# The second MLP of an attention and two-MLP kernel: its TensorE order written out, its token operands double buffered, all weights streamed, and its cosine without a magnitude step

## The chip, the cores and the metric

The kernel runs on one core of a Trainium2 chip. The core has TensorE (PE in the profile; its weight loads are PEld), VectorE (DVE), ScalarE (ACT), GpSimd (POOL) and SyncE (SP, which only issues DMAs here). The metric is the device time of one launch in microseconds; lower is better. The kernel before takes 1585.07 us, the median of three runs (1583.58 to 1586.71).

## The reference

Three stages follow each other: packed attention, an MLP with `h * sigmoid(h)`, and a second MLP with `h * cos(h)`.

```python
p_packed = sm_attn(p, k, v)          # 8 batches, 8 heads, 32 packed queries, 576 keys, head_dim 64
attn_out = sm_attn(q, p_packed, p_packed)
x = attn_out.transpose(0, 2, 1, 3).reshape(4608, 512)

h = x @ w_in                         # first MLP: 512 -> 2048
g = h * (1.0 / (1.0 + np.exp(-h)))
x = g @ w_out                        # 2048 -> 512

h = x @ w_in                         # second MLP, with weights of its own
g = h * np.cos(h)
out = (g @ w_out).astype(np.float32) # 4608 x 512
```

The four weight matrices arrive as 64-bit floats and are decoded on the chip.

## The kernel before

**Arithmetic.** An fp32 operand is split into a rounded part and a remainder, and a product of two such operands is three matmuls into one PSUM bank (`mm3`: remainder times rounded, rounded times remainder, rounded times rounded). `split` makes the two parts: a cast on ACT or DVE, then a subtraction on DVE or POOL.

**Planner.** Nothing is issued when it is written. Every operation is recorded with its cost, its reads and writes (a PSUM bank counts as a whole), and a due time; a list scheduler (`Plan.schedule`, `Plan.order`) then gives each engine one fixed order. Where two engines can do an operation (`either`), the scheduler chooses. Each engine runs its order strictly, so an operation that waits holds up all that stand behind it on that engine. SP issues the DMAs in one such order too.

**First MLP.** 256 steps, each for 288 tokens and 128 of the 2048 hidden columns: six matmuls into a bank `hb`, tanh on ACT, a multiply and a split into `g` on DVE, ACT or POOL, and three steps later twelve matmuls (288 columns wide) into the four banks `acc`. Attention and the decoding of weights run beside it. Its results go to DRAM (`ydram`, and `ypart` for the first two batches, whose sum is made in four parts).

**Second MLP.** Nine blocks of 2 x 256 tokens, eight steps a block, 72 steps in all. A step computes two hidden chunks of 128 columns for both token halves as seven block products instead of eight (`second`). Each product is six matmuls of 256 columns, so a step has 42. `x` and `y` are two PSUM banks of a step: products 0 and 1 go into the halves of x, ACT copies x1 to y1 and x2 to `m`; products 2 and 3 add to y1 and x1, DVE forms x2 = y1 + m; products 4 and 5 add to y1 and x2, DVE forms y2 = y1 + m; product 6 adds to y1. Both banks then go through the cosine (`half_second`): ACT rounds h/2pi to an integer `n`, DVE subtracts that multiple of 2pi in two instructions and clamps, ACT takes the magnitude and then the sine, DVE multiplies by h, and a split gives `g`. The projection of each bank is twelve matmuls of 512 columns into the four banks `acc`, so a step has 24 of them. Steps alternate between two pairs of banks.

**Operands.** The seven token operands of a block (fourteen tiles, `yt`) are sums and differences of four token quarters, loaded from DRAM into `raw` and split (`put` in `load_y`). They lie in a ring of 20 slots, so those of products 0 to 2 of the next block can be made early (`AHEAD_Y = 3`), and the others only in the last step of the block, as each product frees its slots. The weights of product 0 stay on the chip (`held`, eight tiles); those of products 1 to 6 are read again for every block through a ring of 16 slots, 256 KB each (`load_unit`). For three blocks the parts in `ypart` are added first, each through one of two buffers `yad`.

**Order around the change.** Projections get due times 1.6 and 2.1 steps after their step's start, products 0 to 0.95; within these the scheduler interleaves them. `plan.margin = 400` adds 400 ns to what it allows between another engine and TensorE.

## Time and profile before

| | |
|---|---|
| median of three runs | 1585.07 us |
| profiled execution, its own time | 1586.77 us |
| its span, first to last instruction | 1584.7 us |
| PE busy | 1540.7 us, 97% |
| PEld busy | 1378.6 us, 87% |
| DVE busy | 1145.0 us, 72% |
| ACT busy | 857.7 us, 54% |
| POOL busy | 269.0 us, 17% |
| mean granted TensorE clock | 0.991 |

Shares of busy time are means over the whole span. A matmul's duration includes the filling and draining of the array, which overlap with its neighbours, so a dense stretch is read from how far apart matmuls start and not from their durations. Idle time of an engine that nobody waits for costs nothing. Names in the rows: `hb`, `mb`, `sb` are the banks of the products, `acc` those of the projection, `g` the split result of an activation, `r` and `n` the tiles of the cosine, `y` and many `w` tiles hold token operands and weights of the second MLP (tiles that held first-MLP operands are used again). All operations are recorded through one helper, so all stand on one line (L206 before, L207 in the changed kernel).

### The profile page before, as it was taken

What the parts mean: (1) busy time and instruction counts of PE and PEld (TensorE: products, weight loads), DVE (VectorE), ACT (ScalarE), POOL (GpSimd) and SP (SyncE); (2) the same over time, 40 slices, a digit from 0 to 9 for tenths busy, and PEclk for the clock granted to TensorE, in tenths of its full rate; (3) what the DMA queues carried; (4) which work ended last, traced back from release to release, by engine and by line L of the source; (5) the groups of instructions that cost most, each with busy time, mean ns of one, the idle gap of its engine ahead of it and who ended that gap; (6) DMA issues with size and microseconds to landing.
All of it is one profiled execution on the core that took longest, in us unless ns stands there. A gap on an engine that the chain in (4) does not pass through costs nothing.

```text
span 1584.7 us, 31208 instructions
## 1 busy us (share of the span) xinstructions
PE 1540.7 (97%) x11642; PEld 1378.6 (87%) x11642; DVE 1145.0 (72%) x2149; ACT 857.7 (54%) x1798; POOL 269.0 (17%) x294
## 2 busy tenths in 40 slices
PE   9889999999999999999999999999999999999998
PEld 7678878999879998899988898888889898889887
DVE  4997657564787879687657768787777767686766
ACT  5875544344454565556556555555555555555554
POOL 0231001020131303130202203132212102020100
PEclk9899999999999999999999999999999999999999
DMA  9677365222765567565877647666565545464551
GB/s 248 204 227 187 106 146 125 68 46 40 153 210 175 172 175 171 181 202 189 273 245 226 202 147 227 199 191 207 168 186 168 175 151 187 154 186 150 163 164 36
DMA packets 295639, 270.51 MB, mean 171 GB/s; under 512 B 165440, under 2 KB 214080, under 8 KB 295488
## 3 DMA queue, kind: packets, MB, share of 16 engines
q1 hardware_dynamic: 295488, 268.52, 57.1%
q8 instruction: 92, 1.51, 0.4%
q14 instruction: 59, 0.48, 0.1%
HBM read 215.22 MB, written 53.22 MB: 169 GB/s over the span
## 4 chain that ended last, share of the span: by engine, by line
PE 75%; DVE 14%; DMA 4%; ACT 3%; issue 2%; POOL 1%; SPq 1%; DVEq 0%; ACTq 0%; POOLq 0%
PE acc L206 41%; PE hb L206 21%; PE mb L206 7%; PE sb L206 6%; DVE r L206 4%; DVE g L206 1%; DMA yad<-ypart 1%; ACT r L206 1%; DVE w L206 1%; DVE y L206 1%; SPq L206 1%; DVE raw L206 1%; DVE wy L206 1%; DVE wd L206 1%; DVE gf L206 1%
## 5 line engine op out<-in xcount | busy, mean ns | idle before, releaser
L206 PE MATMUL acc<-w,g 128*128 128x512 f32 x1728 | 472.9, 395 | 4.8 <-DVE g L206 4.4
L206 PE MATMUL acc<-g,w 128*128 128x288 f32 x3072 | 470.2, 298 | 4.9 <-ACT ysb L206 3.1
L206 PEld LDWEIGHTS acc<-g,w 128*128 128x128 f32 x3072 | 426.0, 189 | 31.4 <-issue 20.8
L206 PEld LDWEIGHTS acc<-w,g 128*128 128x128 f32 x1728 | 301.1, 189 | 50.2 <-DVE g L206 7.4
L206 PE MATMUL hb<-a,w 128*128 128x288 f32 x1536 | 261.4, 301 | 9.5 <-ACT a L206 3.9
L206 PEld LDWEIGHTS hb<-a,w 128*128 128x128 f32 x1536 | 221.7, 190 | 30.0 <-issue 11.2
L206 PE MATMUL hb<-y,w 128*128 128x256 f32 x1056 | 183.9, 283 | 3.3 <-DVE r L206 2.8
L206 ACT CAST g<-gf 128x288 fp32r<-128x288 f32 x231 | 100.0, 434 | 153.6 <-PE acc L206 114.5
L206 POOL TENSOR_TENSOR g<-gf,g 128x288 fp32r<-128x288 f32 x83 | 82.1, 991 | 546.7 <-ACT g L206 472.2
L206 PEld LDWEIGHTS hb<-y,w 128*128 128x128 f32 x1056 | 161.4, 191 | 14.0 <-DVE r L206 3.6
L206 DVE SCALAR_TENSOR_TENSOR gf<-gf,hb 128x288 f32<-128x288 f32 x256 | 114.0, 447 | 50.6 <-ACT gf L206 49.3
L206 ACT ACTIVATE gf<-hb 128x288 f32<-128x288 f32 x256 | 104.6, 410 | 74.9 <-PE hb L206 67.0
L206 DVE TENSOR_TENSOR g<-gf,g 128x288 fp32r<-128x288 f32 x173 | 83.7, 485 | 83.1 <-ACT g L206 80.3
L206 ACT ACTIVATE r<-r 128x512 f32<-128x512 f32 x144 | 91.0, 632 | 86.1 <-DVE r L206 85.6
L206 DVE TENSOR_TENSOR g<-r,g 128x512 fp32r<-128x512 f32 x135 | 97.5, 722 | 44.6 <-ACT g L206 44.2
L206 ACT CAST g<-r 128x512 fp32r<-128x512 f32 x134 | 83.6, 624 | 71.6 <-DVE r L206 71.2
L206 PE MATMUL hb<-w,w 128*128 128x256 f32 x672 | 117.4, 282 | 2.2 <-DVE r L206 1.3
L206 PEld LDWEIGHTS hb<-w,w 128*128 128x128 f32 x672 | 103.9, 190 | 10.5 <-DVE r L206 1.5
L206 DVE SCALAR_TENSOR_TENSOR r<-n,r 128x512 f32<-128x512 int32 x144 | 105.6, 733 | 3.0
L206 ACT ACTIVATE r<-r,half_pi 128x512 f32<-128x512 f32 x144 | 104.2, 724 | 3.1
L206 ACT ACTIVATE n<-hb 128x512 int32<-128x512 f32 x72 | 43.1, 598 | 88.2 <-PE hb L206 87.9
L206 PE MATMUL mb<-y,w 128*128 128x256 f32 x408 | 74.6, 284 | 2.8 <-DVE hb L206 1.7
(212 smaller groups left out, 2062.8 us busy)
## 6 DMA issues: line engine op xcount, KB each, us to landing
w<-w2s SPq DMA_DIRECT2D x440, 256.0 KB, 3.5
w2s<-wd SPq DMA_DIRECT2D x28, 512.0 KB, 3.6
wd<-in_moe_w_in SPq DMA_DIRECT2D x24, 512.0 KB, 5.0
w<-w1dram SPq DMA_DIRECT2D x48, 256.0 KB, 3.0
wd<-in_moe_w_out SPq DMA_DIRECT2D x20, 512.0 KB, 4.6
ydram<-ysb SPq DMA_DIRECT2D x64, 144.0 KB, 2.9
raw<-ydram SPq DMA_DIRECT2D x72, 128.0 KB, 3.3
w2dram<-wd SPq DMA_DIRECT2D x16, 512.0 KB, 3.0
```

Source lines behind the costliest of these rows:

```text
L206: run = lambda: emit(*[real(x) for x in args], **{k: real(x) for k, x in kw.items()})
```

## The change

1. **Order.** `plan.inorder` makes each matmul of the second MLP wait for the one before it, as written. A written step `s` is: products 0 and 1; the projection of the x bank of step s-2 (twelve matmuls); products 2 and 3; half of the projection of its y bank (six); products 4 and 5; the other half; product 6. Steps 0 and 1 alternate without projections, and two more steps hold the last projections. The margin of 400 ns is no longer set there, and all due times of a step are one. The other engines are still ordered by the scheduler.
2. **Projection inner order.** The twelve matmuls go round the four banks three times (rounded part of `g` times both parts of the weight first, the remainder of `g` last), except for the last hidden chunk. In the first MLP the same is done for all but a block's last chunk.
3. **Token operands.** 28 slots instead of 20, so two blocks fit; all of `put` for a block is recorded at once. The slots come from the weight tiles that held product 0, and from `gf`, `g` and `ysb` tiles of the first MLP (`m`, `yad` and three slots).
4. **Weights.** All seven units of a step are loaded through the same ring of 16 slots.
5. **Cosine.** `n` is rounded from h/2pi + 0.25, so the sine's argument needs no magnitude; one ACT instruction per half step goes. `r`, `g2` and `o` have four buffers (three, three and two before).
6. x takes the banks `mb` and `sb`, y the banks `hb`; two dummy matmuls that opened the y banks go.

```diff
--- before.py
+++ after.py
...
@@ -237,6 +238,9 @@
                 self.block = True
         i = len(self.ops) - 1
         waits = set()
+        if engine == self.PE and self.inorder is not None:
+            waits.update(self.inorder)
+            self.inorder = [i]
         for r in filter(None, ins):
             if r[1] is None:
 
@@ -877,9 +881,10 @@
         PAIR.append(len(steps))
     NS = len(steps)
     LAG = 3
...
@@ -907,9 +912,16 @@
         g = gs()[:, :, :n]
         split(g, t)
         plan.due = due_first(s + LAG + 0.5)
-        for dm in range(KC):
-            c = slice(dm * P, dm * P + P)
-            mm3(acc[dm][:, :n], (W[fc][:, 0, c], W[fc][:, 1, c]), (g[:, 0], g[:, 1]), begin, end)
+        chunks = [slice(dm * P, dm * P + P) for dm in range(KC)]
+        if end:
+            for dm, c in enumerate(chunks):
+                mm3(acc[dm][:, :n], (W[fc][:, 0, c], W[fc][:, 1, c]), (g[:, 0], g[:, 1]), begin, end)
+        else:
+            for dm, c in enumerate(chunks):
+                for j in (1, 0):
+                    T.matmul(acc[dm][:, :n], W[fc][:, j, c], g[:, 0], start=begin and j == 1, stop=False)
+            for dm, c in enumerate(chunks):
+                T.matmul(acc[dm][:, :n], W[fc][:, 0, c], g[:, 1], start=False, stop=False)
         plan.due = None
         if end:
             t0 = k0 // HALF % 2 * (2 * S if part else NT) // 2 + (2 * pr + k0 // S) * HALF
@@ -927,31 +939,27 @@
     order = list(range(3, 6)) + [0, 1, 2] + list(range(6, NBLK))
     wout = {}
     yt = {}
-    X, Y = hb, [mb, sb]
+    X, Y = [mb, sb], hb
 
...
     raws, raw = lates("raw", F32, 10, TB)
-    yads, yad = lates("yad", F32, 2, TB)
-    m5s, m5ring = lates("m5", F32, 2, TB)
-    ys, _ = lates("y", F32R, 12, TB)
+    yad = ring([t[:, :TB] for t in ysb_tiles])
+    m5ring = ring([t[:, :TB] for t in gf_tiles])
+    ys, _ = lates("y", F32R, 9, TB)
     ns, nring = lates("n", I32, 2)
-    rs_, rring = lates("r", F32, 3)
-    g2s, g2ring = lates("g2", F32R, 3)
-    os_, oring = lates("o", F32, 2)
+    rs_, rring = lates("r", F32, 4)
+    g2s, _ = lates("g2", F32R, 4)
+    os_, oring = lates("o", F32, 4)
 
     halves = [W[FC + kc * 4 + s][:, i] for s in range(4) for kc in range(2) for i in range(2)]
     halves += [W[FC + 8 + kc * 4 + s][:, i] for s in range(4) for kc in range(2) for i in range(2)]
...
-    yring = ring(ys + [as_y(x) for x in halves[0:2] + halves[26:32]])
-    held = halves[2:4] + halves[20:26]
-    uring = ring(halves[4:16] + halves[16:20])
-
-    AHEAD_Y = 3
-    later = {}
+    yring = ring(ys + [as_y(x) for x in halves[0:5] + halves[21:32]] + [t[:, :, :TB] for t in g_tiles])
+    uring = ring(halves[5:21])
 
     def load_y(i):
 
...
@@ -1001,71 +1008,103 @@
         DMA.dma_start(f32(w).rearrange("p (k t f) -> p k t f", k=2, t=2), w2s[fp // 4, prod, :, fp % 4])
         return as_w(w)
 
-    def half_second(s, fc, h):
-
-        i = s // FH
+    def cosine(h, g):
+
         n = nring()
-        A.activation(n, h, AF.Copy, scale=INV_2PI / WEIGHT)
+        A.activation(n, h, AF.Copy, scale=INV_2PI / WEIGHT, bias=0.25)
         r = rring()
         V.scalar_tensor_tensor(r, n, -TWO_PI_HI * WEIGHT, h, op0=ALU.mult, op1=ALU.add)
         V.scalar_tensor_tensor(r, n, -TWO_PI_LO * WEIGHT, r, op0=ALU.mult, op1=ALU.add)
-        V.tensor_scalar(r, r, 4.0 * WEIGHT, -4.0 * WEIGHT, op0=ALU.min, op1=ALU.max)
-        A.activation(r, r, AF.Abs)
-        A.activation(r, r, AF.Sin, scale=-1.0 / WEIGHT, bias=half_pi)
+        V.tensor_scalar(r, r, 1.570796 * WEIGHT, -4.7123885 * WEIGHT, op0=ALU.min, op1=ALU.max)
+        A.activation(r, r, AF.Sin, scale=1.0 / WEIGHT, bias=half_pi)
         V.tensor_tensor(r, r, h, ALU.mult)
-        g = g2ring()
         split(g, r)
-        w = wout[fc]
-        last = fc == FC - 1
-        for t in range(4):
-            plan.due = due_second(s + (2.1 if fc >= FH else 1.6))
-            c = slice(t * P, t * P + P)
-            mm3(acc[t], (g[:, 0, c], g[:, 1, c]), (w[:, 0], w[:, 1]), fc == 0, last)
-            plan.due = None
+        return g
+
...
+    gt, st, m5s = {}, {}, {}
+
+    def project(s, x, part):
+
+        if not 0 <= s < NS2:
+            return
+        i, fp = divmod(s, FH)
+        fc = fp + x * FH
+        g, w = gt[s, x], wout[fc]
+        if fc == FC - 1:
+            passes = [(t, a, b) for t in range(4) for a, b in ((1, 0), (0, 1), (0, 0))]
+        else:
+            passes = [(t, 0, b) for b in (1, 0) for t in range(4)] + [(t, 1, 0) for t in range(4)]
+        for n, (t, a, b) in list(enumerate(passes))[6 * part : 6 * part + 6]:
+            first = fc == 0 and n < 4
+            last = fc == FC - 1 and n % 3 == 2
+            T.matmul(acc[t], g[:, a, t * P : (t + 1) * P], w[:, b], start=first, stop=last)
             if last:
-                o = oring()
-                if t % 2:
-                    V.tensor_scalar(o, acc[t], WEIGHT**-2, None, op0=ALU.mult)
-                else:
-                    A.activation(o, acc[t], AF.Copy, scale=WEIGHT**-2)
-                p0 = order[i] * TB + t % 2 * P
-                cuts = [p0] + list(range(p0 // HALF * HALF + HALF, p0 + P, HALF)) + [p0 + P]
-                for a, b in zip(cuts, cuts[1:]):
-                    r0 = a // HALF * S + t // 2 * HALF + a % HALF
-                    DMA.dma_start(out[r0 : r0 + b - a, :], o[a - p0 : b - p0])
-
-    def second(s):
-
-        i, fp = divmod(s, FH)
+                output(i, t)
+
+    def product(s, prod, dst, start=False):
+
+        i = s // FH
+        w = st[s][prod]
+        for c in range(2):
+            b = yt[i, prod, c]
+            mm3(dst, (w[:, c, 0], w[:, c, 1]), (b[:, 0], b[:, 1]), start and c == 0, c == 1, skip_group_check=True)
+
+    def multiply(s, k):
+
+        if s >= NS2:
+            return
         x, y = X[s % 2], Y[s % 2]
         x1, x2, y1, y2 = x[:, :TB], x[:, TB:], y[:, :TB], y[:, TB:]
-        ws = [held[fp]] + [uring() for _ in range(6)]
-        ws = [as_w(ws[0]) if i else load_unit(ws[0], fp, 0)] + [load_unit(w, fp, j) for j, w in enumerate(ws) if j]
-
-        def product(prod, dst, start, due):
-            plan.due = due_second(s + due)
-            for c in range(2):
-                b = yt[i, prod, c]
-                w = ws[prod]
-                mm3(dst, (w[:, c, 0], w[:, c, 1]), (b[:, 0], b[:, 1]), start and c == 0, c == 1, skip_group_check=True)
-            plan.due = None
-            if fp == FH - 1 and i + 1 < NBLK and prod + AHEAD_Y < 7:
-                later[i + 1](prod + AHEAD_Y)
-
-        m5 = m5ring()
-        product(0, x1, True, 0)
-        product(1, x2, False, 0.1)
-        A.copy(y1, x1)
-        A.copy(m5, x2)
-        product(2, y1, False, 0.35)
-        product(3, x1, False, 0.45)
-        V.tensor_tensor(x2, y1, m5, ALU.add)
-        product(4, y1, False, 0.6)
-        product(5, x2, False, 0.7)
-        V.tensor_tensor(y2, y1, m5, ALU.add)
-        half_second(s, fp, x)
-        product(6, y1, False, 0.95)
-        half_second(s, fp + FH, y)
+        if k == 0:
+            st[s] = [load_unit(uring(), s % FH, j) for j in range(7)]
+            m5s[s] = m5ring()
+            product(s, 0, x1, True)
+            product(s, 1, x2)
+            A.copy(y1, x1)
+            A.copy(m5s[s], x2)
+        elif k == 1:
+            product(s, 2, y1)
+            product(s, 3, x1)
+            V.tensor_tensor(x2, y1, m5s[s], ALU.add)
+        elif k == 2:
+            product(s, 4, y1)
+            product(s, 5, x2)
+            V.tensor_tensor(y2, y1, m5s[s], ALU.add)
+            gt[s, 0] = cosine(x, g2s[2 * s % 4])
+        else:
+            product(s, 6, y1)
+            gt[s, 1] = cosine(y, g2s[2 * s % 4 + 1])
+
+    def second(s):
+
+        plan.due = due_second(s)
+        if s == 1:
+            for k in range(4):
+                for x in range(2):
+                    multiply(x, k)
+        elif s > 1:
+            multiply(s, 0)
+            project(s - 2, 0, 0)
+            project(s - 2, 0, 1)
+            multiply(s, 1)
+            project(s - 2, 1, 0)
+            multiply(s, 2)
+            project(s - 2, 1, 1)
+            multiply(s, 3)
+        plan.due = None
 
 
 
@@ -1173,16 +1212,11 @@
         if more:
             seconds(b0 + 3)
 
-    change(top, [att], "yp", "right", raws + yads + m5s + ys)
...
     load_y(0)
-    for prod in range(AHEAD_Y, 7):
-        later[0](prod)
-    for x in Y:
-        yd = yt[0, 0, 0]
-        T.matmul(x[:, :TB], yd[:, 0, :P], yd[:, 0], start=True, stop=True)
-    plan.margin = plan.MARGIN
-    for s in range(NS2):
+    plan.inorder = []
+    for s in range(NS2 + 2):
         i, fp = divmod(s, FH)
         if i == 0:
             for x in range(2):
```

TensorE at a change of block, in the kernel before: the first products of a new block (`y0`, `y1`) into `hb0`, among the last products of the old block into `hb1` and projection matmuls into `acc`.

```order
L206 MATMUL acc0_88<-w2_98,g21_8871 128x512
L206 MATMUL mb_94<-w31_1868,w28_103 128x256
L206 MATMUL hb0_92<-y0_8651,w17_1138 128x256 x3
L206 MATMUL hb0_92<-y1_8652,w17_1138 128x256 x3
L206 MATMUL acc1_89<-w2_98,g21_8871 128x512
L206 MATMUL acc2_90<-w2_98,g21_8871 128x512
L206 MATMUL acc3_91<-w2_98,g21_8871 128x512
L206 MATMUL hb1_93<-y10_8661,w25_1140 128x256
L206 MATMUL hb1_93<-y11_8662,w25_1140 128x256 x2
L206 MATMUL mb_94<-y2_8653,w17_1138 128x256 x3
L206 MATMUL mb_94<-y3_8654,w17_1138 128x256 x3
L206 MATMUL hb1_93<-y11_8662,w25_1140 128x256
```

TensorE in the middle of a step of the changed kernel: products 2 and 3 of the step (into `hb0`, then `mb`), six projection matmuls of the step before the last, then products 4 and 5 begin.

```order
L207 MATMUL hb0_92<-w26_1148,w18_1146 128x256 x3
L207 MATMUL hb0_92<-w30_1149,w18_1146 128x256 x3
L207 MATMUL mb_94<-w30_1149,w22_1147 128x256 x3
L207 MATMUL mb_94<-w27_1838,w22_1147 128x256 x3
L207 MATMUL acc0_88<-w9_1143,g21_8921 128x512
L207 MATMUL acc1_89<-w9_1143,g21_8921 128x512
L207 MATMUL acc2_90<-w9_1143,g21_8921 128x512
L207 MATMUL acc3_91<-w9_1143,g21_8921 128x512
L207 MATMUL acc0_88<-w9_1143,g21_8921 128x512
L207 MATMUL acc1_89<-w9_1143,g21_8921 128x512
L207 MATMUL hb0_92<-w27_1838,w22_1147 128x256 x3
L207 MATMUL hb0_92<-w31_1839,w22_1147 128x256 x3
```

The old order was chosen matmul by matmul; the new one is the written pattern, the same in every step.

DVE in the last step before the same change of block, kernel before: `hb1<-sb,m` and `sb<-sb,m` are the sums x2 and y2, the `r` rows the cosine, and the `raw`, `y0`, `y1` and `y2` rows make the token operands that the block which starts next reads.

```order
L206 SCALAR_TENSOR_TENSOR r1_8868<-n0_8865,hb1_93 128x512
L206 TENSOR_TENSOR sb_95<-sb_95,m51_8650 128x256
L206 SCALAR_TENSOR_TENSOR r1_8868<-n0_8865,r1_8868 128x512
L206 TENSOR_TENSOR raw0_8637<-raw2_8639,raw0_8637 128x256
L206 TENSOR_SCALAR r1_8868<-r1_8868 128x512
L206 TENSOR_TENSOR raw8_8645<-raw6_8643,raw0_8637 128x256
L206 TENSOR_TENSOR y0_8651<-raw0_8637,y0_8651 128x256
L206 CAST y2_8653<-raw8_8645 128x256
L206 CAST y1_8652<-raw1_8638 128x256
L206 TENSOR_TENSOR y2_8653<-raw8_8645,y2_8653 128x256
L206 SCALAR_TENSOR_TENSOR r2_8869<-n1_8866,sb_95 128x512
L206 TENSOR_TENSOR r1_8868<-r1_8868,hb1_93 128x512
```

DVE two steps before the same change of block, changed kernel: the cosine of both banks, among it token operands (`raw`, `w29`, `w30`), and at the end the sum x2 of the next step (`sb<-hb1,gf1`).

```order
L207 TENSOR_TENSOR r0_8916<-r0_8916,mb_94 128x512
L207 SCALAR_TENSOR_TENSOR r1_8917<-n1_8915,r1_8917 128x512
L207 TENSOR_TENSOR raw1_8362<-raw3_8364,raw1_8362 128x256
L207 TENSOR_SCALAR r1_8917<-r1_8917 128x512
L207 TENSOR_TENSOR g20_8920<-r0_8916,g20_8920 128x512
L207 TENSOR_TENSOR w29_1141<-raw0_8361,w29_1141 128x256
L207 TENSOR_TENSOR raw8_8369<-raw6_8367,raw0_8361 128x256
L207 TENSOR_TENSOR r1_8917<-r1_8917,hb0_92 128x512
L207 TENSOR_TENSOR raw3_8364<-raw7_8368,raw3_8364 128x256
L207 CAST w30_1149<-raw4_8365 128x256
L207 TENSOR_TENSOR w30_1149<-raw9_8370,w30_1149 128x256
L207 TENSOR_TENSOR sb_95<-hb1_93,gf1_149 128x256
```

As many token rows as before stand among the cosine rows near a change of block, but in the changed kernel they serve a block that starts eight steps later (their slots have just come free), and the sums x2 and y2 stand right behind the cosine's rows or between token rows.

## Rows read from the trace of the kernel before

**Rows 1.** Chain that ended last: start us, us, what.

```profile
303.32 1.59 PE acc L206 x12
...
990.83 1.92 PE hb L206 x16
...
1297.75 1.61 PE acc L206 x7
```

**Rows 2.** Timeline of PE: start us, us, what, matmuls, idle before.

```profile
790.05 1.59 PE L206 MATMUL hb<-y,w 128*128 128x256 f32 x12
...
1575.27 5.51 PE L206 MATMUL acc<-w,g 128*128 128x512 f32 x23 [0.24 <-DVE g L206]
```

**Rows 3.** Groups by line, 790.3 to 806 us, PE: busy us, mean ns.

```profile
L206 PE MATMUL acc<-g,w 128*128 128x288 f32 x36 | 5.7, 295 | 0.0
```

**Rows 4.** Windows: PE, PEld, DVE, ACT, POOL busy (x), PEclk, DMA, GB/s.

```profile
858.00:898.00 40.00, 37.66 (x222) 33.26 (x221) 32.36 (x58) 21.47 (x43) 14.02 (x17) 0.96 0.64 200
...
898.00:944.00 46.00, 46.00 (x290) 41.46 (x289) 30.93 (x55) 23.86 (x44) 0.92 (x1) 1.00 0.49 160
...
1384.00:1424.00 40.00, 38.24 (x237) 33.74 (x236) 32.73 (x60) 22.15 (x44) 9.82 (x12) 1.00 0.58 179
...
1471.00:1511.00 40.00, 39.80 (x250) 35.77 (x249) 28.68 (x53) 21.13 (x41) 6.07 (x7) 1.00 0.55 172
...
1511.00:1557.00 46.00, 46.00 (x291) 41.51 (x290) 31.16 (x55) 24.95 (x46) 0.00 (x0) 1.00 0.38 121
```

**Rows 5.** Waits of PE from 789 us on: us in total, times, longest.

```profile
PE acc L206 <- DVE g L206: 4.4, 9, 1.8
...
PE hb L206 <- DVE r L206: 4.0, 3, 1.8
...
PE mb L206 <- DVE hb L206: 2.7, 3, 1.0
...
PE hb L206 <- DVE hb L206: 1.5, 2, 0.9
```

**Rows 6.** Timeline, 879 to 888 us: POOL, DVE and PE.

```profile
879.59 1.86 POOL L206 TENSOR_TENSOR raw<-raw,yad 128x256 f32<-128x256 f32 x2
...
880.79 1.21 DVE L206 TENSOR_TENSOR g<-r,g 128x512 fp32r<-128x512 f32 x1
...
882.05 1.79 PE L206 MATMUL acc<-w,g 128*128 128x512 f32 x5 [1.78 <-DVE g L206]
```

**Rows 7.** Groups by line, whole span: busy us, mean ns, idle before.

```profile
L206 ACT ACTIVATE n<-hb 128x512 int32<-128x512 f32 x72 | 43.1, 598 | 88.2 <-PE hb L206 87.9
...
L206 DVE SCALAR_TENSOR_TENSOR r<-n,hb 128x512 f32<-128x512 int32 x72 | 49.2, 684 | 16.6 <-ACT n L206 16.1
...
L206 DVE SCALAR_TENSOR_TENSOR r<-n,r 128x512 f32<-128x512 int32 x144 | 105.6, 733 | 3.0
...
L206 DVE TENSOR_SCALAR r<-r 128x512 f32<-128x512 f32 x144 | 68.3, 475 | 3.2
...
L206 ACT ACTIVATE r<-r 128x512 f32<-128x512 f32 x144 | 91.0, 632 | 86.1 <-DVE r L206 85.6
...
L206 ACT ACTIVATE r<-r,half_pi 128x512 f32<-128x512 f32 x144 | 104.2, 724 | 3.1
...
L206 DVE TENSOR_TENSOR r<-r,hb 128x512 f32<-128x512 f32 x72 | 49.2, 684 | 11.9 <-ACT r L206 11.4
...
L206 ACT CAST g<-r 128x512 fp32r<-128x512 f32 x134 | 83.6, 624 | 71.6 <-DVE r L206 71.2
...
L206 DVE TENSOR_TENSOR g<-r,g 128x512 fp32r<-128x512 f32 x135 | 97.5, 722 | 44.6 <-ACT g L206 44.2
...
L206 DVE TENSOR_TENSOR hb<-mb,m 128x256 f32<-128x256 f32 x36 | 15.4, 428 | 9.0 <-PE hb L206 8.8
```

**Rows 8.** Waits of PE up to 789 us.

```profile
PE acc L206 <- POOL g L206: 1.8, 2, 1.4
```

**Rows 9.** DMA issues: count, KB each, median us to landing.

```profile
w<-w2s SPq DMA_DIRECT2D x440, 256.0 KB, 3.5
```

More of the change, by code (lines that the diff above doesn't have):

```diff
@@ L107, in __init__ @@
         self.margin = 0
+        self.inorder = None
         self.block = None
@@ L879, in attention_mlps_kernel @@
     LAG = 3
-    gfs = ring(tiles(gp, [P, TA], F32, "gf", 2))
-    gs = ring(tiles(gp, [P, 2, TA], F32R, "g", LAG))
-    ysbs = ring(tiles(gp, [P, TA], F32, "ysb", 2))
+    gf_tiles = tiles(gp, [P, TA], F32, "gf", 2)
+    g_tiles = tiles(gp, [P, 2, TA], F32R, "g", LAG)
+    ysb_tiles = tiles(gp, [P, TA], F32, "ysb", 2)
+    gfs, gs, ysbs = ring(gf_tiles), ring(g_tiles), ring(ysb_tiles)
     def first(s):
@@ L990, in put @@
                 split(yt[i, prod, c], x[c])
-        for prod in range(AHEAD_Y):
+        for prod in range(7):
             put(prod)
-        later[i] = put
     def load_wout2(c, w):
@@ L1037, in second, with output @@
-    def second(s):
-        i, fp = divmod(s, FH)
+        return g
+    def output(i, t):
+        o = oring()
+        if t % 2:
+            V.tensor_scalar(o, acc[t], WEIGHT**-2, None, op0=ALU.mult)
+        else:
+            A.activation(o, acc[t], AF.Copy, scale=WEIGHT**-2)
+        p0 = order[i] * TB + t % 2 * P
+        cuts = [p0] + list(range(p0 // HALF * HALF + HALF, p0 + P, HALF)) + [p0 + P]
+        for a, b in zip(cuts, cuts[1:]):
+            r0 = a // HALF * S + t // 2 * HALF + a % HALF
+            DMA.dma_start(out[r0 : r0 + b - a, :], o[a - p0 : b - p0])
@@ L1057, in second @@
-        product(1, x2, False, 0.1)
-        A.copy(y1, x1)
-        A.copy(m5, x2)
-        product(2, y1, False, 0.35)
-        product(3, x1, False, 0.45)
-        V.tensor_tensor(x2, y1, m5, ALU.add)
-        product(4, y1, False, 0.6)
-        product(5, x2, False, 0.7)
-        V.tensor_tensor(y2, y1, m5, ALU.add)
-        half_second(s, fp, x)
-        product(6, y1, False, 0.95)
-        half_second(s, fp + FH, y)
+        if k == 0:
[14 more added lines that the diff above has]
+            gt[s, 0] = cosine(x, g2s[2 * s % 4])
+        else:
+            product(s, 6, y1)
+            gt[s, 1] = cosine(y, g2s[2 * s % 4 + 1])
@@ L1174, in attention_mlps_kernel @@
             seconds(b0 + 3)
-    change(top, [att], "yp", "right", raws + yads + m5s + ys)
+    change(top, [att], "yp", "right", raws + ys)
     change(mid, [a2p], "cp", "left", ns + rs_ + g2s + os_)
     load_y(0)
-    for prod in range(AHEAD_Y, 7):
-        later[0](prod)
-    for x in Y:
-        yd = yt[0, 0, 0]
-        T.matmul(x[:, :TB], yd[:, 0, :P], yd[:, 0], start=True, stop=True)
-    plan.margin = plan.MARGIN
-    for s in range(NS2):
+    plan.inorder = []
+    for s in range(NS2 + 2):
         i, fp = divmod(s, FH)
```

## The prediction

> **What bounds the kernel now.** I read the chain that ended last first: PE holds 75% of it, most of that in the projection banks `acc` and the product banks `hb`, and its dense pieces give PE's pace [rows 1]: twelve matmuls of 288 columns in 1.59 us are 132.5 ns each, sixteen of 256 columns in 1.92 us are 120 ns, seven of 512 columns in 1.61 us are 230 ns. Then the timeline of PE gives the ends of the second MLP [rows 2]: its first product starts at 790.05 us, and the last 23 matmuls start at 1575.27 and take 5.51, so it ends at 1580.78. That is 790.7 us.
>
> What must fit there: a step has 42 product matmuls (42 x 0.120 = 5.04 us) and 24 projection matmuls (24 x 0.230 = 5.52), together 10.56 us, and 72 steps are 760.3 us. In the same stretch lie 36 matmuls left over from the first MLP [rows 3], 36 x 0.1325 = 4.8 us, and two dummies, 0.24. Sum 765.3. So PE loses 790.7 - 765.3 = 25.4 us in the second MLP, and this is all that a better order there can win.
>
> Where it loses them, the windows say [rows 4]. Between changes of block PE is busy in every microsecond (46.00 of 46 in the first such stretch and in the last). In the 40 us around a change it is idle for 2.34 us at the first (40 - 37.66), 1.76 at the one near 1404 and 0.20 at the last. DVE and POOL show why: in the quiet stretch DVE is busy 30.93 of 46 us, a rate of 0.67, and POOL 0.92 in all; around a change DVE has 32.36 and 32.73 of 40, where 0.67 x 40 = 26.9 would do, and POOL 14.02 and 9.82. The token operands of the next block are made there, 5 to 6 us of DVE work too much in one place. PE's waits name the victims [rows 5]: 4.4 us for the split `g` that a projection needs, 4.0 for the `r` instruction that frees a product bank, 2.7 and 1.5 for the sums x2 and y2. These four are 12.6 us; refilling after each stall, a clock that is down after the worst one (0.96 in that window [rows 4]) and shorter gaps make up the rest of the 25.4.
>
> **The written order, step by step.** Count from a step's start in dense time: products 0 and 1 end at 1.44 us, the projection of the x bank at 4.20, products 2 and 3 at 5.64, six projection matmuls at 7.02, products 4 and 5 at 8.46, six more at 9.84, product 6 at 10.56.
>
> *Waits that go.* A projection now reads a `g` whose bank was complete in the step before the last. Its chain is n 0.598, r 0.684 and 0.733, clamp 0.475, sine 0.724, product 0.684, cast 0.624, remainder 0.722 [rows 7], in all 5.24 us. With hand-offs that is some 5.5 us, and the projection asks for it 14.1 us after the x bank is complete (2.10 + 10.56 + 1.44) and 16.2 after the y bank (10.56 + 5.64). So the 4.4 us for `g` go. A bank is needed again a full step after it is complete, against about 4 us up to the multiply by h: the 4.0 us for `r` go too. Token operands were made for the very next step in the old order; now they are a block ahead, 84 us, so no product waits for them. The two ACT copies have 2.76 us of projection as cover, and each takes well under a microsecond even behind a sine of 0.724.
>
> *Waits that stay.* Three things per step are still awaited within it: the copies, x2 and y2. Each sum takes 0.428 us on DVE [rows 7], and six projection matmuls, 1.38 us, cover x2 (y2 has products 5 and these). This cover holds if DVE is free in time. DVE's row of x2 stands behind the whole cosine of the step before, and that gives a loop: chain 5.24 us, hand-offs 0.25 (eight, an estimate from neighbouring rows of 0.03 each), about 0.5 for the x bank's rows in between (an estimate: one row of 0.684 that has begun), x2 0.43, then on PE products 4 and 5 1.44, six projections 1.38, product 6 0.72 and its drain 0.15 (twelve matmuls of 0.12 take 1.59 [rows 2]). That is 10.1 us. PE's own step is 10.56. So in a quiet step PE sets the pace and 0.45 us are to spare. The removed magnitude instruction is 0.632 us [rows 7] of this loop: with it the loop would have been 10.7, over PE's step. As ACT work alone it would be worth nothing, since ACT is idle nearly half of the time.
>
> *Changes of block.* DVE still makes the token operands in a bunch, now in the steps in which their slots come free; there are seven such bunches (blocks 2 to 8), each over two to three steps. The 5.5 us of extra work [rows 4] fall partly into DVE's own idle time (between x2 and y2 it waits 1.3 us for PE, and 0.9 before the next cosine), partly into the loop. By the order about half are in the loop, six of them in the row of instructions shown before x2. Half is 2.75 us over two steps, less 2 x 0.45 to spare, so 1.85 us of stall at each, say 1.8. Bounds: 0 if all of it falls into idle time, 4.6 (5.5 - 0.9) if all is in the loop. I take the middle since the order shows token rows on both sides. Seven times 1.8 is 12.6 us; two refills each at 0.1 add 1.4.
>
> *The rest of the stretch.* The start, where the last first-MLP matmuls fill the gaps of steps 0 and 1, and the three blocks with `yad` additions: 2 us together, 0 to 5. The two dummies: minus 0.24. The end: before, the last 23 matmuls waited 0.24 [rows 2]; now 24 matmuls of the step before last (5.52 us) and twelve of the x bank (2.76) cover the last y chain of 5.5, so nothing is gained or lost.
>
> *Weights.* 64 loads more of 256 KB (440 become 504), 16.8 MB in 791 us or 21 GB/s, beside the 121 to 200 of the windows [rows 4]. A load is issued when its slot comes free, 16 units or 2.3 steps (24 us) before its use, and lands in 3.5 us [rows 9]. SP's queue also holds the `yad` loads, which wait for POOL; one such wait can delay weights by a few us, and 20 are there. Cost 0, at most 3.
>
> *First MLP.* The remainder of `g` is asked for four matmuls later than before, 0.53 us. What waited there for POOL's remainder is 1.8 us in two waits [rows 8]. The scheduler also lays out the whole first part anew. I take -1, from -4 to +5 (the evictions of `acc` get shorter notice where a block begins).
>
> *Sum.* Of 25.4 us lost, 12.6 + 1.4 + 2 = 16.0 remain, so 9.4 are won, plus 1 in the first MLP: 10.4. The profiled execution took 1586.77 us (span 1584.7 and 2.1 around it), so 1576.4; it was 1.7 above the median, 1585.07, which gives 1574.7 there. I predict 1575 us.
>
> One row speaks against it. While POOL ran two additions of 1.86 us together, a DVE remainder took 1.21 us instead of 0.722, and PE's wait of 1.78 us ended with it [rows 6]. The bunches keep some twelve POOL operations, and a strict order passes each such delay on. The stretched time is already in DVE's busy time in the windows, so the sum holds it once. The Trainium skill, page "SBUF — State Buffer", section "Who interferes with whom", says that a DVE instruction with two SBUF inputs and a GpSimd instruction that reads SBUF take one port pair by an exclusive lock, so that the later one is blocked for the whole of the other. The trace agrees in direction, with half a microsecond and not a whole POOL operation. By the page each collision of an 0.93 us addition would cost up to 0.93.
>
> **Rivals.**
> - *All of it goes.* The bunches fall into DVE's idle time, since nothing that a bunch makes is urgent any more. For it: DVE has 3.4 us idle in a step (10.56 x 0.33). Against it: in a fixed order unurgent work still stands before urgent work. Then 4 us remain of 25.4: 1585.07 - 21.4 - 1 = 1562.7.
> - *No change.* Three of the twelve POOL operations of a bunch stretch a DVE row inside the loop by 0.5 us each, on top of the 1.8: 3.3 a bunch, 23.1, and with 2 for the rest all 25 are lost again: 1584 to 1585. For it: [rows 6]; against it: these stretches are partly counted already.
> - *Slower: DVE's loop becomes the pace of every step.* The place is x2 in each step, PE standing before product 4. The price is 72 times what the loop exceeds 10.56. Against the 25.4 lost before, it decides from a loop of 10.91 on. At 11.0 it costs 72 x 0.44 = 31.7, 6.3 more than before: 1591. For it: the spare time of 0.45 rests on hand-offs of 0.03 us and on n for the y bank never waiting behind a copy or sine on ACT. Against it: the loop would have to be 0.9 longer than its rows.
> - *The order does not hold.* If the scheduler left PE idle in its layout, or a weight came late, the stalls would show on DMA. It would cost a few us and is in the range.
>
> **How the numbers follow.** My forecast (1568 to 1581) has 0.45, all of it goes 0.25, no change 0.15, the slower loop 0.12, and 0.03 are left for a late transfer or a worse first MLP. This kernel's measurement can tell 0.2%, 3.2 us. Faster by that (under 1581.9) are nearly all of the forecast and the first rival and a little of the second: 0.72. Same: 0.14. Slower: 0.14. The range takes in the first rival and most of the third: 1560 to 1589.
>
> **What the profile afterwards would show.** Right: the stretch from the first product to the last matmul about 781 us instead of 790.7; windows between changes of block dense as before; PE's waits for `g` and for the `r` that frees a bank gone; what is left waits for DVE's sums, seven groups of them, near steps 6 to 8 of a block. All gone would show no wait for DVE at all. Slower would show a short wait for x2 in each of 70 steps, PE idle evenly in all windows. Wrong in its parts: waits for a weight's DMA, or a first MLP that ends more than 5 us away from where it does now.

## The result, and the profile after

The changed kernel takes 1599.3 us (1597.47 to 1602.48, four runs) against 1584.32 (1582.41 to 1586.71, four) for the kernel before: ratio 1.0096, 95% interval 1.0074 to 1.0118. It is slower by 15 us, where 1575 was forecast, and lies above the range. The profiled spans are 1595.7 and 1584.7 us, and the 11 us between them are all lost in the second MLP.

The ends of the second MLP in TensorE's timeline of the changed kernel (start us, us, what, matmuls), which answer to [rows 2]:

```profile
782.77 0.40 PE L207 MATMUL mb<-y,w 128*128 128x256 f32 x2
...
1582.73 9.00 PE L207 MATMUL acc<-w,g 128*128 128x512 f32 x39
```

The stretch is 1591.73 - 782.77 = 808.96 us. It holds the 72 steps (760.3 us) and 88 first-MLP matmuls still to do (counted in the trace; 11.7 us; 36 before [rows 3]), 772.0 together. TensorE loses 37.0 us in it, for 25.4 before: 11.6 more. The first part came out even: the first product starts 7.3 us earlier, but 52 more matmuls are left, 6.9 us.

TensorE's waits from 789 us on (us in total, times, longest), against [rows 5]:

```profile
PE hb L207 <- DVE sb L207: 18.7, 9, 2.5
PE hb L207 <- DVE mb L207: 5.4, 8, 1.3
PE acc L207 <- ACT ysb L207: 0.2, 1, 0.2
```

The waits for `g` (4.4 us) and for `r` (4.0) are gone. What is left waits for x2, the sum that opens the way for products 4 and 5 (it is written to `sb` or `mb`, by turns). Windows (PE, PEld, DVE, ACT, POOL busy, PEclk, DMA, GB/s) of a first and a late change of block, of a quiet stretch between, and of the late change cut in three, against [rows 4]:

```profile
862.00:902.00 40.00, 37.24 (x229) 32.54 (x228) 34.03 (x62) 18.73 (x38) 14.09 (x15) 1.00 0.74 233
...
1350.00:1390.00 40.00, 40.00 (x251) 36.11 (x250) 26.44 (x47) 16.30 (x32) 0.00 (x0) 1.00 0.58 187
1394.00:1418.00 24.00, 21.53 (x127) 19.28 (x127) 21.41 (x36) 12.08 (x26) 10.87 (x12) 0.93 0.46 144
```

```profile
1396.00:1406.70 10.70, 8.29 (x51) 7.11 (x49) 10.62 (x18) 5.46 (x13) 7.05 (x8) 0.99 0.50 162
1406.70:1409.50 2.80, 2.74 (x13) 2.74 (x14) 2.80 (x6) 1.21 (x3) 2.35 (x3) 0.50 0.03 9
1409.50:1412.00 2.50, 2.50 (x15) 2.18 (x15) 2.29 (x5) 0.96 (x2) 0.73 (x1) 0.92 0.61 188
```

Quiet steps are dense. At a change of block DVE is busy for 10.62 of 10.70 us with only 18 instructions, and POOL runs beside it. The stall, in TensorE's timeline:

```profile
1402.74 1.55 PE L207 MATMUL acc<-w,g 128*128 128x512 f32 x6
1406.76 1.01 PE L207 MATMUL hb<-y,w 128*128 128x256 f32 x3 [2.47 <-DVE sb L207]
...
1409.49 1.75 PE L207 MATMUL acc<-w,g 128*128 128x512 f32 x6
```

The six projections end their pace at 1402.74 + 6 x 0.23 = 1404.12; product 4 starts 2.64 us later. After these 2.47 us of idle time the clock is granted at 0.50, the level of 1.2 GHz, and the next twelve matmuls take 2.73 us (to 1409.49) for 1.44. With some 0.4 us a step later that is about 4.4 us. The same stall of 2.64 to 2.68 us stands at 866, 956, 1048, 1137, 1226, 1315 and 1404 us: seven, one in each bunch. The clock falls at six of them and not at the first, which costs 3.4 us in all; the seven together cost 30.8. Four smaller ones (1.2 to 1.5 us, 812 to 1026 us) make up most of the rest.

What DVE did in front of that x2 (`sb<-hb,gf`), and POOL beside it, both in the changed kernel:

```profile
1398.00 0.69 DVE L207 SCALAR_TENSOR_TENSOR r<-n,hb 128x512 f32<-128x512 int32 x1
...
1399.22 1.02 DVE L207 SCALAR_TENSOR_TENSOR r<-n,r 128x512 f32<-128x512 int32 x1
1400.16 0.95 DVE L207 TENSOR_TENSOR raw<-raw,raw 128x256 f32<-128x256 f32 x1
...
1401.37 1.23 DVE L207 TENSOR_TENSOR g<-r,g 128x512 fp32r<-128x512 f32 x1
1402.53 0.95 DVE L207 TENSOR_TENSOR y<-raw,y 128x256 fp32r<-128x256 f32 x1
1403.40 0.96 DVE L207 TENSOR_TENSOR raw<-raw,raw 128x256 f32<-128x256 f32 x1
...
1405.22 0.81 DVE L207 CAST y<-raw 128x256 fp32r<-128x256 f32 x1
...
1406.29 0.42 DVE L207 TENSOR_TENSOR sb<-hb,gf 128x256 f32<-128x256 f32 x1
1406.62 0.87 DVE L207 TENSOR_TENSOR g<-r,g 128x512 fp32r<-128x512 f32 x1
```

```profile
1398.07 1.62 POOL L207 TENSOR_TENSOR y<-raw,y 128x256 fp32r<-128x256 f32 x2 [73.94 <-DVE y L207]
1399.65 1.18 POOL L207 TENSOR_TENSOR raw<-raw,raw 128x256 f32<-128x256 f32 x1
1401.19 0.86 POOL L207 TENSOR_TENSOR raw<-raw,raw 128x256 f32<-128x256 f32 x1 [0.36 <-DVE raw L207]
...
1406.11 1.98 POOL L207 TENSOR_TENSOR y<-raw,y 128x256 fp32r<-128x256 f32 x2 [0.23 <-DVE y L207]
```

Undisturbed, these shapes take 0.69 (512 columns), 0.41 (256) and 0.29 us (cast). Six rows are 0.33, 0.54, 0.54, 0.54, 0.55 and 0.52 us too long, 3.0 us in all: more than the whole stall. What a row between SBUF tiles gains is what is left of POOL's row when it starts, less 0.14 us (0.10 to 0.18 in 91 of the 92 such rows with over 0.3 us left): at 1399.22, 1400.16 and 1401.37 POOL's rows have 0.47, 0.67 and 0.68 us left, and the DVE rows gain 0.33, 0.54 and 0.54. A row that reads a PSUM bank is not lengthened: x2 starts at 1406.29, 0.18 us behind POOL's row, and keeps its 0.42 us. Before two of the four smaller stalls one row does the harm: the clamp at 918.89 and the one at 1022.30 take 1.52 us for 0.43, each beside one POOL remainder of `g` of 1.35 us.

### The profile page after: what moved, and what is told of

Same layout as the page of the kernel before. It is cut to its first block, busy times and chain, and to the rows that moved or that the text cites. A ratio compares the mean times of both kernels' runs of the same rounds, so it can differ in the third digit from the quotient of the medians.

```text
span 1595.7 us, 31482 instructions
## 1 busy us (share of the span) xinstructions
PE 1544.8 (97%) x11640; PEld 1384.5 (87%) x11640; DVE 1150.4 (72%) x2140; ACT 780.6 (49%) x1663; POOL 270.3 (17%) x294
## 4 chain that ended last, share of the span: by engine, by line
PE 72%; DVE 17%; DMA 4%; ACT 2%; issue 2%; SPq 1%; POOL 0%; DVEq 0%; ACTq 0%; POOLq 0%
PE acc L207 38%; PE hb L207 18%; PE sb L207 8%; PE mb L207 8%; DVE r L207 5%; DVE g L207 2%; DVE w L207 2%; DVE wy L207 1%; DVE raw L207 1%; DVE wd L207 1%; SPq L207 1%; DMA wd<-in_moe_w_in 1%; DMA wd<-in_moe_w_out 1%; DVE gf L207 1%; ACT g L207 1%
## 5 line engine op out<-in xcount | busy, mean ns | idle before, releaser
L207 PE MATMUL acc<-g,w 128*128 128x288 f32 x3072 | 475.9, 297 | 5.9 <-ACT ysb L207 3.6
L207 PEld LDWEIGHTS acc<-g,w 128*128 128x128 f32 x3072 | 426.8, 188 | 36.6 <-issue 21.3
L207 PE MATMUL acc<-w,g 128*128 128x512 f32 x1728 | 434.9, 394 | 0.2 <-ACT ysb L207 0.2
L207 PEld LDWEIGHTS acc<-w,g 128*128 128x128 f32 x1728 | 313.6, 190 | 56.4 <-ACT ysb L207 0.7
L207 PE MATMUL hb<-a,w 128*128 128x288 f32 x1536 | 271.8, 304 | 10.9 <-DVE gf L207 4.3
L207 POOL TENSOR_TENSOR g<-gf,g 128x288 fp32r<-128x288 f32 x105 | 99.7, 951 | 510.6 <-PE acc L207 269.0
L207 DVE TENSOR_TENSOR g<-gf,g 128x288 fp32r<-128x288 f32 x151 | 71.8, 476 | 69.1 <-PE acc L207 43.1
L207 DVE TENSOR_TENSOR hb<-hb,gf 128x256 f32<-128x256 f32 x72 | 31.0, 431 | 68.6 <-PE hb L207 68.4
L207 ACT ACTIVATE n<-mb 128x512 int32<-128x512 f32 x36 | 21.5, 598 | 109.3 <-PE mb L207 109.3
L207 PEld LDWEIGHTS hb<-y,w 128*128 128x128 f32 x360 | 53.4, 191 | 24.3 <-DVE sb L207 13.1
L207 PE MATMUL hb<-y,w 128*128 128x256 f32 x360 | 58.2, 287 | 14.6 <-DVE sb L207 10.9
```

The source lines that it names most:

```text
L207: run = lambda: emit(*[real(x) for x in args], **{k: real(x) for k, x in kw.items()})
```

## The experiments

Each was run with the kernel before on the same chip; ratios are to it. "Lost" is TensorE's time in the second MLP beyond dense, worked out as above.

**GpSimd barred from the second MLP.** Theory: POOL's running beside DVE makes the stalls.

```diff
-                combine(st[:, :n], st[:, :n], ad[:, :n], ALU.add)
+                V.tensor_tensor(st[:, :n], st[:, :n], ad[:, :n], ALU.add)
 ...  (the token differences and both remainders likewise: VectorE only)
```

> The changed kernel with GpSimd barred from the second MLP: token operands, the additions of parts and the remainders of g are all made on VectorE, some 14 to 19 rows of 0.41 us more in each bunch. In the row of instructions before the sum x2 at a change of block as many token rows stand as before (five or six). Theory 1 (GpSimd's operations, running beside VectorE's, stretch its rows in the loop from 0.41 to 0.95 us and from 0.72 to 1.23): the stall of 2.64 us before product 4 at each of the seven bunches falls under 1.5 us, PE's lost time in the second MLP from 37 to about 20 us, the time from 1599 to about 1582. Theory 2 (the number of token rows in VectorE's fixed order, whatever their length): the stall stays at 2.6 us or grows, the lost time is 37 to 60 us, the time 1599 to 1620.

1567.02 us, ratio 0.9871 (0.9851 to 0.9891): 32 us faster than the changed kernel, faster than before, lost 4.3. Theory 1 had the direction right, but forecast 17 us of these 32. Its waits:

```profile
PE hb L207 <- DVE sb L207: 2.1, 5, 0.7
PE hb L207 <- DVE mb L207: 1.9, 2, 1.4
```

DVE does all the token work itself, yet comes in time. In 16 us of a bunch it does 39 instructions (below, the kernel without GpSimd there):

```profile
1375.00:1391.00 16.00, 16.00 (x103) 14.54 (x102) 15.96 (x39) 9.82 (x22) 0.00 (x0) 1.00 0.51 167
```

**No token work** (operands made for the first two blocks only, then reused, so later blocks get the wrong tokens):

```diff
+        if i > 1:
 ...  (yt[i, prod, c] = yt[i - 2, prod, c] for all, and no loads, sums or splits)
```

> The changed kernel that makes token operands only for the first two blocks and uses these for all nine, so the output is not the reference's: no loads of tokens, no additions and no bunches from block 2 on. Theories 1 and 2 (bunches of token work): PE's lost time in the second MLP falls from 37 to 4 to 7 us, the time to 1565 to 1570. Theory 3 (the written TensorE order stalls by itself, in every step, because VectorE's loop is as long as PE's step): over 20 us stay lost, the time stays over 1582.

1562.23 us, ratio 0.9845 (0.9817 to 0.9873), nothing lost. The written order is dense by itself; without the token work, and so without POOL beside it there, the stalls are gone.

**Bunch spread** (the operands of product p are planned behind step p of the block before; they wait for the last matmul written for that step, not for its start; POOL allowed):

```diff
-        for prod in range(7):
-            put(prod)
+        later[i] = put
 ...  (called once a step, behind that step's last matmul)
```

> The changed kernel with the token operands of a block spread: those of product n of the next block are planned behind the start of step n of a block (n from 0 to 6), one pair per step instead of all in the two steps in which the slots come free. GpSimd still takes its share. Theories 1 and 2: the stalls of 2.64 us go, since a step then has two to four token rows; PE's lost time in the second MLP 37 to 6 to 12 us, the time 1567 to 1575, faster than the kernel before too. Theory 3: no change, 1599.

1585.9 us (ten runs), ratio 0.9996 (0.9983 to 1.0009), lost 21.3. The expectation missed: the seven big stalls are gone, but some 48 small ones (0.1 to 1.3 us) come instead. POOL now meets DVE more often: 129 DVE rows of the second MLP are lengthened by over 0.1 us beside it, 44.9 us together, for 95 rows and 44.6 us in the changed kernel. The two largest waits:

```profile
PE hb L208 <- DVE mb L208: 5.0, 8, 1.0
PE hb L208 <- DVE sb L208: 4.0, 10, 1.1
```

**The old cosine, with its magnitude, in the changed kernel:**

```diff
-        A.activation(n, h, AF.Copy, scale=INV_2PI / WEIGHT, bias=0.25)
+        A.activation(n, h, AF.Copy, scale=INV_2PI / WEIGHT)
 ...
+        A.activation(r, r, AF.Abs)
```

> The changed kernel with the cosine as it was before (rounding without the offset, a magnitude on ScalarE of 0.63 us, sine). By the loop of the prediction (10.1 us of PE's 10.56 in a quiet step) it would be 10.7: quiet steps stall by 0.1 to 0.2 us each, 60 of them give 6 to 12 us, and each bunch 0.6 more, 4 us: 1609 to 1615. Rival: the loop has room, or ScalarE's work hides, and the time stays at 1599 within 3 us.

1597.28 us, ratio 1.0068 (1.0046 to 1.009), lost 37: the same within the measurement, as the rival had it. In the bunches the magnitude does cost: the seven big stalls are 3.0 to 3.6 us there. But the three small ones at 922, 1014 and 1026 us are gone, so the total does not tell its price. A quiet stretch is dense with it, too:

```profile
1340.00:1390.00 50.00, 50.00 (x314) 45.21 (x313) 34.81 (x61) 26.65 (x49) 0.00 (x0) 1.00 0.63 201
```

**Idle GpSimd work put beside the first experiment's kernel**, all rows of PE, DVE and ACT unchanged:

```diff
+                G.tensor_tensor(scratch, f32(y[:, 0]), f32(y[:, 1]), ALU.subtract)
+                plan.ops[-1].cost = 0
```

> The kernel with GpSimd barred from the second MLP (1567 us, 4.1 us lost in its second MLP), with one idle GpSimd subtraction (128x256, result used by nothing) behind each of the 14 token operands of a block; the order of the instructions on TensorE, VectorE and ScalarE is the same, row for row. Theory, that GpSimd's running beside it stops VectorE: some 14 x 0.9 us of GpSimd work fall among VectorE's rows in each bunch, these are lengthened by 0.4 to 0.6 us each as they were in the changed kernel, the stall of over 2 us before the fifth product comes back at each of the seven late bunches, and the time is 1585 to 1605 us. Rival, that the written order or the scheduler's placing of the token work is what counts, or that VectorE waited for GpSimd's results (no result is waited for here): within 3 us of 1567.

1605.41 us (two runs), ratio 1.0113 (1.0093 to 1.0134): 38 us more, and no engine waits for the added results. The stall before the fifth product (product 4) is back (2.41 to 2.43 us beyond dense in each of the seven bunches), and in 16 us of one DVE gets 29 instructions done, for 39 above:

```profile
1408.00:1424.00 16.00, 14.87 (x88) 12.12 (x86) 16.00 (x29) 8.30 (x19) 7.44 (x10) 1.00 0.46 148
```

Timeline of DVE without the added work, then with it, then POOL's with it:

```profile
1379.37 0.42 DVE L207 TENSOR_TENSOR raw<-raw,raw 128x256 f32<-128x256 f32 x1
1379.70 0.42 DVE L207 TENSOR_TENSOR y<-raw,y 128x256 fp32r<-128x256 f32 x1
1380.04 0.42 DVE L207 TENSOR_TENSOR hb<-hb,gf 128x256 f32<-128x256 f32 x1
1380.37 1.08 DVE L207 TENSOR_TENSOR y<-raw,y 128x256 fp32r<-128x256 f32 x3
```

```profile
1412.69 0.95 DVE L207 TENSOR_TENSOR raw<-raw,raw 128x256 f32<-128x256 f32 x1
1413.56 0.96 DVE L207 TENSOR_TENSOR y<-raw,y 128x256 fp32r<-128x256 f32 x1
1414.45 0.42 DVE L207 TENSOR_TENSOR hb<-hb,gf 128x256 f32<-128x256 f32 x1
1414.78 2.12 DVE L207 TENSOR_TENSOR y<-raw,y 128x256 fp32r<-128x256 f32 x3
```

```profile
1412.57 1.67 POOL L207 TENSOR_TENSOR scratch<-y 128x256 f32<-128x256 f32 x2 [2.36 <-DVE y L207]
1414.67 0.74 POOL L207 TENSOR_TENSOR scratch<-y 128x256 f32<-128x256 f32 x1 [0.42 <-DVE y L207]
1415.82 2.61 POOL L207 TENSOR_TENSOR scratch<-y 128x256 f32<-128x256 f32 x3 [0.42 <-DVE y L207]
```

The same rows in the same order take 0.95 for 0.42 and 2.12 for 1.08 us; the row that starts between two of POOL's operations and reads a PSUM bank keeps its 0.42. Over the execution POOL has 96.2 us more (246.9 for 150.7) and DVE 46.5 more (1183.6 for 1137.1): half a microsecond of DVE for each of POOL. This pair shows that GpSimd's running beside VectorE makes the stalls by itself.

**The kernel before, with GpSimd barred from its second MLP** (the same edits).

> The kernel before with GpSimd barred from its second MLP (token sums and differences and the remainders of g all on VectorE), nothing else changed. It tells how much of the 1567 us is owed to the change itself. If GpSimd caused most of the 25 us that TensorE lost there: 1563 to 1570 us, and the change is worth nothing on its own. If single buffered token operands and the scheduler's order caused them, as the prediction had it: 1578 to 1586 us, and the change is worth 10 to 20 us once GpSimd is out of the way. In between I would expect 1573, since the waits for g and for r are not all behind a GpSimd operation.

1564.71 us, ratio 0.9862 (0.9825 to 0.9899). Beside 0.9871 for the changed kernel: once GpSimd is out, the change is worth nothing that can be measured.

**The planner charges the whole overlap.**

```diff
-    SHARED = 0.5
+    SHARED = 1.0
```

> The changed kernel with one number of the planner changed: it charges a VectorE operation between SBUF tiles the whole of GpSimd's remaining time instead of half of it (SHARED 1.0 for 0.5), in the whole kernel. Theory, that the planner undercounts the stretch and so puts the multiply's second sum behind too much token work: it now sees the delay and the seven stalls shrink, TensorE loses 10 to 25 us in the second MLP for 36.8, 1577 to 1592 us. Rival: which engine gets an operation is chosen by the bare costs, so GpSimd still gets its share, the stretch stays, and the time is 1595 to 1603.

1596.2 us, ratio 1.0059 (1.0043 to 1.0074). The rival held: the choice of engine does not look at this number, so POOL keeps its work and the stalls stay (20.2 us for `sb`).

**GpSimd barred everywhere, in the changed kernel, then in the kernel before, then in the changed kernel with the scheduler's order:**

```diff
     def combine(dst, x, y, op):
-        with plan.either():
-            V.tensor_tensor(dst, x, y, op)
-            G.tensor_tensor(dst, x, y, op)
+        V.tensor_tensor(dst, x, y, op)
```

> GpSimd barred from every sum and difference of the whole kernel, the attention and the first MLP too (105 remainders of g of 0.95 to 0.99 us there in the changed kernel, which take about 0.4 us on VectorE). If its running beside VectorE costs there as it does in the second MLP: 1545 to 1563 us, with less TensorE time lost before 789 us. If VectorE, busy 70% before 789 us, has no room in some stretch: 1567 to 1580.

> The kernel before with GpSimd barred from every sum and difference, in all its stages, as the changed kernel was for 1545.8 us (ratio 0.974). Barred in the second MLP alone, before and changed kernel came out alike (0.986 and 0.987). If the change itself (written order, double buffered tokens, shorter cosine) is worth nothing once GpSimd is out: ratio 0.971 to 0.976, 1541 to 1549 us. If it is worth some microseconds that the earlier pair could not tell: 1549 to 1556.

> The changed kernel with GpSimd barred everywhere (1545.8 us, some 4 to 5 us lost by TensorE in the second MLP) and with the written TensorE order given up: the scheduler orders the second MLP's matmuls by their due steps, as in the kernel before. Theory, that the strict order neither wins nor costs once the sums come in time: 1542 to 1550. Rival, that the scheduler fills the last 4 to 5 us with other products: 1538 to 1542; or that it puts worse stalls in than the written order has: over 1552.

1545.76 us (ratio 0.9737, 0.9719 to 0.9756), 1538.56 (0.9712, 0.9686 to 0.9738) and 1537.63 (0.97, 0.9674 to 0.9726). All three beat both kernels, and their intervals overlap. TensorE loses 4.9 us in the second MLP of the first, 2.2 in that of the second and nothing in that of the third, so the scheduler's order fills the last few us, as the rival of the third run had it. In the second of them TensorE's first product comes at 766.5 us with 24 first-MLP matmuls left, for 790.05 with 36: the first part wins some 22 us too.

**The scheduler's order in the changed kernel, GpSimd allowed; then its two halves apart.**

```diff
-    plan.inorder = []
+    plan.margin = plan.MARGIN
```

So the scheduler's order comes with its margin of 400 ns. Of the two halves the first run keeps both lines, the second has neither.

> The changed kernel, GpSimd allowed as there, with the written TensorE order given up for the scheduler's. It tells why the same GpSimd work cost the kernel before 25 us and the changed kernel 37 us. If the strict order is what turns each late sum into a stall (nothing may be put in front of the waiting product): 1580 to 1590 us. If the scheduler has as little to put there, since it plans with sums that come in time, and the seven operands issued at once are the cause: 1595 to 1605.

> The changed kernel, GpSimd allowed and the written TensorE order kept, with one line added: the planner plans every result for TensorE 400 ns later, as it did in the second MLP of the kernel before (the margin went with the scheduler's order when the change was made). If the margin is what brought the run with the scheduler's order to 1568.5 us: 1568 to 1580. If the strict order makes the stalls: 1592 to 1602, since in a written order no margin moves TensorE's rows, and only VectorE's order shifts a little.

> The changed kernel, GpSimd allowed, with the scheduler's TensorE order and without the 400 ns margin. If the strict order makes the stalls: 1568 to 1578, little more than with the margin. If the margin does the work: 1585 to 1600. If each does a part: between, 1578 to 1585, and the other run between 1580 and 1592.

1568.54 us (ratio 0.9896, 0.9869 to 0.9922), lost 11: below both ranges of its expectation. Strict order with the margin: 1597.68 (1.0057, 1.0037 to 1.0078). Scheduler's order without it: 1601.18 (1.0086, 1.0066 to 1.0105). Neither half does anything alone; I had expected one of them to do nearly all. Waits with the scheduler's order and the margin, then without the margin:

```profile
PE hb L207 <- DVE hb L207: 2.5, 4, 0.8
PE hb L207 <- DVE mb L207: 1.9, 3, 1.3
```

```profile
PE hb L207 <- DVE sb L207: 14.0, 6, 2.5
PE hb L207 <- ACT hb L207: 8.8, 13, 1.7
```

A late change of block with both (POOL busy, TensorE dense):

```profile
1366.00:1386.00 20.00, 20.00 (x125) 17.70 (x124) 19.29 (x39) 12.15 (x27) 8.14 (x9) 1.00 0.56 184
```

POOL still runs for 8.1 us there, but its delay no longer reaches TensorE. The median time from the end of x2 to product 5, the first to add to its bank, is 1.26 us in the changed kernel, 1.25 with the margin alone, 1.63 with the scheduler's order and the margin, and 0.95 without the margin: only in a free order does the margin move the product. DVE's rows are also lengthened less with both, by 30 us in the second MLP for 45 in the changed kernel.

## Why the prediction was wrong

**The step that failed** is the price of a bunch under "Changes of block", and the sentence below the sum: "The stretched time is already in DVE's busy time in the windows, so the sum holds it once." A bunch was priced by the amount of DVE work, half of 5.5 us less what is to spare, 1.8. Measured are 2.64 of stall and, with the half clock and the refill, 4.4 on the mean of the seven, where 1.8 and 0.2 for refills stood: seven times the difference of 2.4 is 17 of the 21 us by which the loss was underestimated (37.0 for 16.0), and the four smaller stalls, 5.2 us where 2 stood, are most of the rest. The amount of work was not the cause. With POOL barred DVE does more token work in each bunch and the stalls go (lost 4.3); with idle POOL work added to that very order they return. The 5 to 6 us of "work too much" read from [rows 4] were mostly stretch, which depends on which rows POOL meets: in the window at 858 us of the kernel before nine DVE rows are 4.4 us too long together beside POOL, in the one near 1404 eight rows 3.6 us. In the changed kernel it meets six rows before one x2.

**The row that spoke against it was read, and priced too low.** [Rows 6] had the mechanism, 1.21 us for 0.722. The rival "no change" took three such stretches a bunch at 0.5; six came, 3.0 us. The size of one was right (0.52 to 0.55, one of 0.33). The Trainium skill, page "SBUF — State Buffer", section "Who interferes with whom", has the later of the two blocked until the other ends. The runs agree but for a constant: a row gains what is left of POOL's operation, less 0.14 us. The same section exempts DVE rows with at most one SBUF input, outside the modes that use both ports, and says that a cast can enter such a mode. The trace agrees for x2, whose other input is in PSUM (0.42 us at 1406.29); the cast at 1405.22, with one input, was lengthened (0.81 for 0.29), and no row shows which mode it ran in.

**What the price hangs on was missed.** The change gave up two things the prediction passed over, the freedom of the order and the 400 ns margin. The text knew that "a strict order passes each such delay on", but put no price on it. With both back, the same kernel runs at 0.9896 of the kernel before, inside the range; with one of them, it stays slow. So the 31 us between 1599.3 and 1568.5 belong to the two together.

**The loop** was sized rightly for the changed kernel, and the price of the magnitude was not. In a quiet step x2 stands behind the second bank's whole cosine, as was summed; it ends at 1361.39 us, and product 4 starts 0.58 us later, where 0.45 to spare was forecast (a product that waits starts 0.05 us behind its sum):

```profile
1360.37 0.69 DVE L207 TENSOR_TENSOR g<-r,g 128x512 fp32r<-128x512 f32 x1 [0.69 <-ACT g L207]
1360.97 0.42 DVE L207 TENSOR_TENSOR sb<-hb,gf 128x256 f32<-128x256 f32 x1
```

```profile
1361.97 0.52 PE L207 MATMUL hb<-y,w 128*128 128x256 f32 x3
```

With the magnitude it was to be 10.7 us, over TensorE's step of 10.56, at 72 x 0.14 = 10 us. But the loop has no fixed order: with the magnitude in the kernel the scheduler puts x2 in front of that remainder of `g` (60 times, for 9 in the changed kernel), and quiet steps stay dense:

```profile
1360.24 0.43 DVE L207 TENSOR_TENSOR sb<-hb,gf 128x256 f32<-128x256 f32 x1 [0.31 <-PE sb L207]
1360.62 0.69 DVE L207 TENSOR_TENSOR g<-r,g 128x512 fp32r<-128x512 f32 x1
```

The rival that ended slower stood on this loop in every step: x2 was the right place, but it stalls in the bunches and not in quiet steps.

**Right:** the waits for `g` and for `r` went; all that is left but 0.2 us waits for DVE's sums, most of it in seven groups; quiet steps are dense; the first part is even (-0.4); no wait for a weight's DMA shows, the 64 loads more landing in the same time as [rows 9]:

```profile
w<-w2s SPq DMA_DIRECT2D x504, 256.0 KB, 3.6
```

**Open:** what of the 16 us that the changed kernel with the scheduler's order wins on before is owed to the double buffered operands and what to the rest was not run apart. Why the margin helps only a free order is shown in part: it moves product 5 there and not in the written order. Which matmuls then fill the time, and what the smaller stretch of DVE's rows gives, was not tried apart.

## What to carry to other kernels

Read a helper engine's price off the rows of the engine beside it, not off its own. Here GpSimd did some 120 us of sums in the second MLP (270.3 us busy, and 150.7 where it was barred there) and lengthened VectorE's rows in front of TensorE; barring it from all sums made the kernel before 2.9% faster (0.9712) and the changed kernel 3.6% (0.9737 for 1.0096). And an order written out by hand takes away the scheduler's means to absorb a late result: before doing so, count for each awaited result how late it may come, with every row in front of it at its disturbed length.

## What the runs showed that was not expected

Two kernels that differ by 15 us with GpSimd are alike without it (0.9862 and 0.9871). And a stall can cost more than itself: near 1406 us the clock fell to the level of 1.2 GHz for 2.8 us and more, and the twelve matmuls in it took 1.3 us longer. It is not so after every stall. In the changed kernel the clock fell at six of the seven stalls of 2.47 to 2.51 us of idle time and not at the first, and not at those of 1.0 to 1.3 us. With the idle GpSimd work it fell at three of seven stalls of 2.25 to 2.28 us. The stretch behind the first big stall of the changed kernel and that behind the fifth:

```profile
868.80:871.80 3.00, 3.00 (x18) 2.48 (x18) 3.00 (x5) 1.66 (x4) 2.30 (x4) 1.00 0.55 184
1229.20:1232.00 2.80, 2.80 (x13) 2.80 (x14) 2.76 (x5) 1.22 (x3) 2.27 (x4) 0.50 0.37 128
```

What tells the two apart was not tried.
